# Loading the output projection in runs of 4 KiB, with the attention output laid out to match

## The chip, the cores and the metric

The kernel runs on one core of one Trainium2 chip. The metric is the device time of one execution in microseconds (us); medians of several runs are given. In the lines of the profile, PE is TensorE's matmul unit, DVE is VectorE, ACT is ScalarE, and SPq is the queue of SyncE, which issues the loads. The loads are carried by 16 DMA engines.

## The reference, cut to what matters

```python
xn  = layernorm(x)                               # x: 4 x 1 x 512
q   = (xn @ wq) as (4, 32 heads, 1, 128)
p   = softmax(q . k_cache * 128**-0.5)           # k_cache: 4 x 32 x 8192 x 128, bf16
o   = p . v_cache                                # v_cache: the same size
out = x + o.reshape(4, 1, 4096) @ wo + ffn(xn)   # wo: 4096 x 512
```

One decode step for a batch of 4: K and V together are 537 MB, wo is 4.19 MB, and all of it is read once.

## The kernel before: the parts that the argument touches

K and V come in tiles of 2 MiB through a pool of nine slots, all issued from one queue, one K and one V tile for each of the 128 (head, batch) pairs. After the four batches of a head, its output stands in PSUM with one row per batch and group; it is copied to SBUF, *turned* so that the 128 values of the head lie on the partitions, divided by the row sums, and later multiplied with the 128 rows of wo that belong to the head.

```python
def load_wo(half):                       # two tiles of 16 heads; runs of 512 elements = 1 KiB
    n = H // 2
    t_ = slot()
    nc.sync.dma_start(out=t_[:].rearrange("p (h e) -> p h e", h=n),
                      in_=A_wo[half * n * P:(half + 1) * n * P, :].rearrange("(h p) e -> p h e", p=P))
    wo_t.append(t_)
...
def fin_2(h):                            # the turn: 4 fp32 matmuls with 128 stationary columns
    o_sb = osb.pop(h)
    xps = psX.tile([P, B], dt.float32, name="xps")
    for u in range(NV):
        mm(xps[:], o_sb[:, u * Dh:(u + 1) * Dh], ident_f[:, u:P:QB], start=(u == 0))
    nc.vector.tensor_tensor(out=otn[:, h, :], in0=xps[:], in1=rcp.pop(h)[:], op=ALU.mult)

def wo_mm(h):                            # one product per head, added up in PSUM
    w = wo_t[h // (H // 2)][:].rearrange("p (h e) -> p h e", e=D)
    mm(yo_ps[0:B, :], otn[:, h, :], w[:, h % (H // 2), :], start=False)
...
        if 0 <= mf < M and mf % B == B - 1:
            fin_2(mf // B)
            wo_ready = mf // B + 1       # products of wo that may be issued
```

## Time and profile before

| what | before |
|---|---|
| time, median of 6 runs | 1297.78 us (1297.59 to 1297.96) |
| share of the span in which PE was busy | 85% |
| read from HBM | 550.77 MB |
| rate in most slices | 429 to 434 GB/s |
| rate in slices 36 and 37 (the wo loads) | 403 and 419 GB/s |
| PE passes in the turn of all heads | 256, 253 ns each |

So there are two numbers to read from any run of it: **when the last K tile lands**, and **how long the chain behind it is**. The lines of the profile itself stand in the prediction.

### The profile page before, as it was taken

What the parts mean: (1) busy time and instruction counts of PE and PEld (TensorE: products, weight loads), DVE (VectorE), ACT (ScalarE), POOL (GpSimd) and SP (SyncE); (2) the same over time, 40 slices, a digit from 0 to 9 for tenths busy, and PEclk for the clock granted to TensorE, in tenths of its full rate; (3) what the DMA queues carried; (4) which work ended last, traced back from release to release, by engine and by line L of the source; (5) the groups of instructions that cost most, each with busy time, mean ns of one, the idle gap of its engine ahead of it and who ended that gap; (6) DMA issues with size and microseconds to landing.
All of it is one profiled execution on the core that took longest, in us unless ns stands there. A gap on an engine that the chain in (4) does not pass through costs nothing.

```text
span 1295.9 us, 11245 instructions
## 1 busy us (share of the span) xinstructions
PE 1095.1 (85%) x4676; PEld 423.2 (33%) x4676; DVE 693.3 (54%) x887; ACT 48.5 (4%) x102; POOL 5.6 (0%) x11
## 2 busy tenths in 40 slices
PE   5889888888888888888888888888888888886987
PEld 2343333333333333333333333333333333332333
DVE  7635554554554565555565455555555555544542
ACT  1000000000000000000000000000000000000000
POOL 1000000000000000000000000000000000000000
PEclk8989999999999999999999999999989989998999
DMA  9999999999999999999999999999999999999997
GB/s 396 429 430 432 431 429 431 431 431 430 430 432 430 430 430 431 431 429 432 432 428 429 434 430 429 431 431 431 431 431 431 430 430 431 430 403 419 432 429 305
DMA packets 42210, 551.49 MB, mean 426 GB/s; under 512 B 4264, under 2 KB 8368, under 8 KB 8880
## 3 DMA queue, kind: packets, MB, share of 16 engines
q1 hardware_dynamic: 42160, 550.79, 99.6%
q8 instruction: 36, 0.59, 0.2%
q14 instruction: 14, 0.11, 0.0%
HBM read 550.77 MB, written 0.00 MB: 425 GB/s over the span
## 4 chain that ended last, share of the span: by engine, by line
DMA 91%; PE 5%; DVE 3%; issue 0%; SPq 0%; ACT 0%; DVEq 0%; ACTq 0%
DMA slot<-in_A_k_cache_dram 86%; DMA slot<-in_B_w_up_dram 3%; DVE kt L256 3%; DMA slot<-in_A_v_cache_dram 3%; PE oacc L74 2%; PE sps L74 2%; PE mps L74 1%; PE xps L74 0%; SPq L97 0%; PE mps L278 0%; SPq L89 0%; DVE mx L272 0%; DVE res L388 0%; DVE yfx L227 0%; ACT o_sb L313 0%
## 5 line engine op out<-in xcount | busy, mean ns | idle before, releaser
L256 DVE STREAM_TRANSPOSE kt<-slot 128x1024 uint32<-128x1024 uint32 x512 | 593.5, 1212 | 284.8 <-DMA slot<-in_A_k_cache_dram 284.8
L74 PE MATMUL sps<-kt,zq 128*128 128x512 bf16 x2048 | 572.1, 416 | 179.0 <-DVE kt L256 165.6
L74 PEld LDWEIGHTS <-zq 128*128 128x128 bf16 x2048 | 208.8, 103 | 532.0 <-issue 361.4
L302 DVE RECIPROCAL rcp<-mps 128x4 f32<-128x4 f32 x32 | 5.8, 183 | 160.9 <-PE mps L74 160.9
L272 DVE TENSOR_REDUCE mx<-sps 128x1 f32<-128x512 f32 x32 | 22.1, 692 | 45.1 <-PE sps L74 45.1
L281 DVE TENSOR_REDUCE nm<-mps 128x4 f32<-128x64 f32 x32 | 7.2, 225 | 50.0 <-PE mps L278 50.0
L74 PE MATMUL xps<-ident_f,o_sb 128*128 128x4 f32 x256 | 33.1, 253 | 0.7 <-ACT o_sb L313 0.7
L74 PEld LDWEIGHTS xps<-ident_f,o_sb 128*128 128x128 f32 x256 | 31.1, 192 | 1.2 <-ACT o_sb L313 1.2
L247 DVE COPY zq<-qt 32x16 bf16<-32x16 bf16 x128 | 23.5, 183 | 1.3
L322 DVE TENSOR_TENSOR otn<-xps,rcp 128x4 bf16<-128x4 f32 x32 | 5.2, 162 | 34.1 <-PE xps L74 34.1
L313 ACT COPY o_sb<-oacc 128x512 f32<-128x512 f32 x32 | 18.7, 585 | 20.6 <-PE oacc L74 20.5
L74 PE MATMUL oacc<-slot,pt__1952 128*4 128x512 bf16 x64 | 14.6, 379 | 0.0
L74 PE MATMUL oacc<-slot,pt__3394 128*4 128x512 bf16 x64 | 14.6, 379 | 0.0
L74 PE MATMUL oacc<-slot,pt__6498 128*4 128x512 bf16 x64 | 14.6, 379 | 0.0
L74 PE MATMUL oacc<-slot,pt__922 128*4 128x512 bf16 x64 | 14.6, 379 | 0.0
L74 PE MATMUL oacc<-slot,pt__2158 128*4 128x512 bf16 x64 | 14.6, 379 | 0.0
L74 PE MATMUL oacc<-slot,pt__3188 128*4 128x512 bf16 x64 | 14.6, 379 | 0.0
L74 PE MATMUL oacc<-slot,pt__4424 128*4 128x512 bf16 x64 | 14.6, 379 | 0.0
L74 PE MATMUL oacc<-slot,pt__5248 128*4 128x512 bf16 x64 | 14.6, 379 | 0.0
L74 PE MATMUL oacc<-slot,pt__6282 128*4 128x512 bf16 x64 | 14.6, 379 | 0.0
L74 PE MATMUL oacc<-slot,pt__371 128*4 128x512 bf16 x64 | 14.6, 379 | 0.0
L74 PE MATMUL oacc<-slot,pt__1128 128*4 128x512 bf16 x64 | 14.6, 379 | 0.0
(204 smaller groups left out, 636.8 us busy)
## 6 DMA issues: line engine op xcount, KB each, us to landing
slot<-in_A_k_cache_dram SPq DMA_DIRECT2D x128, 2048.0 KB, 38.4
slot<-in_A_v_cache_dram SPq DMA_DIRECT2D x127, 2048.0 KB, 38.8
slot<-in_A_wq_dram SPq DMA_DIRECT2D x2, 2048.0 KB, 9.4
slot<-in_A_wo_dram SPq DMA_DIRECT2D x2, 2048.0 KB, 28.8
slot<-in_A_v_cache_dram SPq DMA_DIRECT2D x4, 512.0 KB, 28.0
slot<-in_B_w_gate_dram SPq DMA_DIRECT2D x1, 1792.0 KB, 38.2
slot<-in_B_w_up_dram SPq DMA_DIRECT2D x1, 1792.0 KB
slot<-in_B_w_down_dram SPq DMA_DIRECT2D x1, 1792.0 KB, 34.0
```

Source lines behind the costliest of these rows:

```text
L74: nc.tensor.matmul(out_ap, lhsT=lhsT, rhs=rhs, start=start, stop=True, skip_group_check=True, **kw)
L247: nc.vector.tensor_copy(out=zq[h % 2][a * QB:(a + 1) * QB, :, :, XO + a * QB].rearrange("p b (j r) -> p r j b", r=2), in_=qt[a * QB:(a + 1 ...
L256: nc.vector.transpose(out=kt[:].bitcast(dt.uint32).rearrange("p (j t r) -> p t j r", j=2, r=QB), in_=src.rearrange("p (t j r) -> p t j r", ...
L272: nc.vector.reduce_max(out=mx[:], in_=s_ps[h][:], axis=AX.X)
L281: nc.vector.tensor_reduce(out=nm[:], in_=mps[:, 0:P].rearrange("p (a x g r) -> p x a g r", a=NQ, x=B, r=2)[:, :, :, :, 0], axis=AX.XY, op= ...
L302: nc.vector.reciprocal(out=r_[:], in_=mps[:, P:P + B])
L313: nc.scalar.copy(out=o_sb[:], in_=o_acc[h % 2][:])
L322: nc.vector.tensor_tensor(out=otn[:, h, :], in0=xps[:], in1=rcp.pop(h)[:], op=ALU.mult)
```

## The change

The intent is larger runs for wo: a partition gets four neighbouring rows of wo, 4 KiB, instead of one of 1 KiB. Partition p then holds the rows 4p to 4p+3 of a block of 512 rows, which belong to head p // 32 of the block and to its elements 4(p mod 32) to +3. The attention output has to lie the same way: 32 partitions for each of four heads, every fourth element per product. So the turn makes 16 narrow matmuls in place of 4 wide ones, and the products of four heads can start only when all four are there.

```diff
-        nc.sync.dma_start(out=t_[:].rearrange("p (h e) -> p h e", h=n),
-                          in_=A_wo[...].rearrange("(h p) e -> p h e", p=P))
+        nc.sync.dma_start(out=t_[:].rearrange("p (k c e) -> p k (c e)", c=4, e=D),
+                          in_=A_wo[...].rearrange("(k p c) e -> p k (c e)", p=P, c=4))
 ...
-        xps = psX.tile([P, B], dt.float32, name="xps")
-        for u in range(NV):
-            mm(xps[:], o_sb[:, u * Dh:(u + 1) * Dh], ident_f[:, u:P:QB], start=(u == 0))
-        nc.vector.tensor_tensor(out=otn[:, h, :], in0=xps[:], in1=rcp.pop(h)[:], op=ALU.mult)
+        xps = psX.tile([P, 4, B], dt.float32, name="xps")
+        k, hh = divmod(h, 4)
+        q0, q1 = hh * QB, (hh + 1) * QB
+        for c in range(4):
+            for u in range(NV):
+                mm(xps[q0:q1, c, :], o_sb[:, u * Dh + c:(u + 1) * Dh:4], ident_f[:, u:P:QB], start=(c == 0 and u == 0))
+        nc.vector.tensor_tensor(out=otn[q0:q1, k * 4:k * 4 + 4, :], in0=xps[q0:q1],
+                                in1=rcp.pop(h)[q0:q1, :].unsqueeze(1).to_broadcast([QB, 4, B]), op=ALU.mult)
 ...
-            wo_ready = mf // B + 1
+            wo_ready = mf // B // 4 * 4 + (4 if mf // B % 4 == 3 else 0)
```

## The prediction

> **What bounds the kernel now.** I read the page first: the slices, the chain that ended last, and the DMA issues.
>
> ```profile
> span 1295.9 us, 11245 instructions
> ...
> DMA  9999999999999999999999999999999999999997
> GB/s 396 429 430 432 431 429 431 431 431 430 430 432 430 430 430 431 431 429 432 432 428 429 434 430 429 431 431 431 431 431 431 430 430 431 430 403 419 432 429 305
> DMA packets 42210, 551.49 MB, mean 426 GB/s; under 512 B 4264, under 2 KB 8368, under 8 KB 8880
> ...
> DMA 91%; PE 5%; DVE 3%; issue 0%; SPq 0%; ACT 0%; DVEq 0%; ACTq 0%
> ...
> slot<-in_A_wo_dram SPq DMA_DIRECT2D x2, 2048.0 KB, 28.8
> ```
>
> The reader is to see that the 16 DMA engines are busy in every slice and that the chain is 91% DMA: 550 MB have to come in, nearly all of it K and V, and they do so at 431 GB/s. PE is 85% busy, but its idle time is spent waiting for transposed K, which waits for the loads. Two dips stand out in the rate: the first slice (start-up) and slices 36 and 37 (403 and 419), where the two wo tiles of 2 MiB are loaded. The change cannot touch the first. So I looked at the second with a table of busy time in stretches of 4 us around the wo loads (its last two columns are the DMA engines' busy share and GB/s), and at what the issuing queue did then.
>
> ```profile
> 1130.00:1150.00 20.00, 16.21 (x69) 5.93 (x67) 11.76 (x18) 1.36 (x3) 0.00 (x0) 1.00 1.01 431
> ...
> 1154.00:1158.00 4.00, 3.15 (x19) 1.82 (x18) 1.00 (x3) 0.00 (x0) 0.00 (x0) 1.00 1.03 404
> 1158.00:1162.00 4.00, 3.45 (x9) 1.23 (x9) 3.88 (x4) 0.00 (x0) 0.00 (x0) 0.58 0.84 290
> 1162.00:1166.00 4.00, 4.00 (x19) 1.47 (x18) 0.00 (x0) 0.00 (x0) 0.00 (x0) 0.99 0.99 381
> ...
> 1174.00:1178.00 4.00, 4.00 (x15) 1.40 (x14) 2.67 (x6) 0.00 (x0) 0.00 (x0) 0.79 1.11 379
> ```
>
> ```profile
> 1128.83 0.39 SPq L236 DMA_DIRECT2D slot<-in_A_wo_dram  x1
> 1131.53 29.54 SPq L97 DMA_DIRECT2D slot<-in_A_k_cache_dram  x1
> 1161.16 0.38 SPq L106 DMA_DIRECT2D slot<-in_A_v_cache_dram  x1
> 1161.64 0.39 SPq L236 DMA_DIRECT2D slot<-in_A_wo_dram  x1
> 1162.12 14.25 SPq L97 DMA_DIRECT2D slot<-in_A_k_cache_dram  x1
> ```
>
> The lasting rate is 431 GB/s. The eight stretches from 1150 to 1182 us moved 424, 404, 290, 381, 430, 420, 379 and 397: together 323 GB/s short, times 4 us, over 431, is **3.0 us lost** around wo. That is the ceiling of the gain. 0.16 x 4 = 0.64 us of it, in 1158 to 1162, is engines with nothing to do (share 0.84): the K load issued behind the first wo load took 29.54 us to issue against the usual 0.33, so the queue behind wo ran nearly dry. The other 2.36 us are engines that were busy and moved less.
>
> The end matters as much, because a single core's time ends with it. The timeline of the last 16 us:
>
> ```profile
> 1278.99 1.03 PE L74 MATMUL xps<-ident_f,o_sb 128*128 128x4 f32 x8
> ...
> 1280.28 0.38 PE L74 MATMUL yo_ps<-slot,otn 128*4 128x512 bf16 x1 [0.25 <-DVE otn L322]
> ...
> 1284.21 6.21 PE L74 MATMUL oacc<-slot,pt__6913 128*4 128x512 bf16 x32 [0.32 <-DMA slot<-in_A_v_cache_dram]
> ...
> 1291.16 1.05 PE L74 MATMUL xps<-ident_f,o_sb 128*128 128x4 f32 x8 [0.73 <-ACT o_sb L313]
> ```
>
> From 1284.21 on PE never waits for data again: 32 matmuls with V, a copy by ACT, the 8 passes that turn the last head, one DVE multiply, one product with wo, the cast and the store. Every nanosecond added to the last head's turn or to the wo products behind it is on the path. What is added for head 30 (at 1278.99) has 0.32 us to spare.
>
> **What the Trainium skill says.** "DMA: Bandwidth & Descriptors", section "Why small descriptors are slow (HBM only)", gives a fixed overhead of about 3 cycles per packet beside 32 bytes per cycle. An estimate from it: 1 KiB takes 35 cycles instead of 32, 9% more; 4 KiB 131 instead of 128, 2% more. On 9.73 us of wo (4.19 MB at 431 GB/s) that is 0.9 and 0.2 us. The trace agrees in kind, but its loss of 2.36 us is larger, so I use the trace. "TensorE: Matmul & The Clock Gate", section "LDWEIGHTS (loading the stationary operand)", has the load as columns / 1.2 ns, whatever the rows: 107 ns for 128 columns, 27 for 32. The trace agrees for 128: eight passes in 1.03 us, the last lasting 0.25, leave 0.78 / 7 = 111 ns per pass. No row of this trace has 32 fp32 columns. The same page, "Weight-path perf modes", says that the fast weight load needs 128 weights that are not fp32; these are fp32, so going to 32 columns should lose no fast load. "TensorEngine Tiling (Array Packing)", section "Key Properties", says that a change of tiling mode drains TensorE; the kernel already goes between 128-column and 4-column matmuls without a wait beyond some tenths of a us, so I charge nothing for it.
>
> **The change part by part.** Load: each wo tile goes from 2048 runs of 1 KiB to 512 of 4 KiB. Per engine, both tiles are 4096 / 16 = 256 packets; 2.36 us / 256 = 9.2 ns extra per packet. With 64 packets that leaves 0.6 us, so 1.77 us come back. The dry queue should go too, as K's issue has a quarter of wo's packets ahead of it: 0.64 us. **Gain 2.4 us**, and it reaches the end, since the transposes after wo still wait for K (4.40 us before the one at 1225.94, 5.15 us before the one at 1264.84).
>
> The turn of a head: 4 fp32 matmuls (8 passes) with 128 stationary columns become 16 (32 passes) with 32 columns at a stride of 4 elements. The build confirms 16 where there were 4, with the other engines' sequences unchanged. At 111 ns the old passes take 0.89 us. For the new ones the shortest spacing in the trace is about 27 ns (24 matmuls with 16 columns moving, 0.76 us less the last one's time), and the strided bf16 weights of the FFN take 3.52 / 56 = 63 ns. I choose the middle, 45 ns: 32 x 45 = 1.44 us, so **+0.55 us per head** (0 to +1.1). For 32 heads that is 18 us of PE, but all save the last two lie where PE idles for K: its matmuls for the scores have 179 us of idle time ahead of them. DVE's multiply writes 32 x 16 instead of 128 x 4; it lasts 162 ns now, and 12 more elements per partition are an estimated 0.01 to 0.02 us.
>
> The wo products: four heads now have to be there before any of the four is used, so those of heads 28, 29 and 30 move behind head 31. One costs (1.24 - 0.38) / 4 = 0.215 us from the run of five at 1207.80. **At the end +0.65 us.** In return head 30's product and PE's wait of 0.25 us for it leave 1280.28, 0.47 us in all, about what that head's longer turn adds; the 0.32 us of slack takes the rest.
>
> Sum: -2.4 + 0.0 (head 30) + 0.55 (head 31) + 0.65 = **-1.2 us**, so 1297.76 - 1.2 = 1296.6 us.
>
> **The rivals.** First, the turn becomes slow: if narrow strided loads do not overlap with matmuls, a pass takes its whole 250 ns, 32 of them 8 us. That would be +7 us per head, +14 at the end, 1310 us. Against it: the 4-column loads of the V products already run ahead of matmuls, 3.11 us for 16. In the middle it would still be mostly hidden, since PE has some 2.5 us to spare in each 9.7 us that a K and a V load need, and a head is turned once in four of those. Second, the loads gain nothing: 4 KiB runs may be as slow as 1 KiB ones, or the loss may be of two large tiles ahead of K in the queue, not of the run length. Then only the end's cost is left: 1299. For it: nothing in the middle of the trace has 4 KiB runs. Against it: the last V is loaded in four parts of 4 KiB runs and its slice still moved 429 GB/s before the ramp down. Third, the whole 3.0 us come back and the turn costs nothing: 1295.4.
>
> **Range and chances.** The best case is -3.0 + 0.65 = -2.35 us; a poor one is -1.0 + 0.65 + 1.1 + 0.3 (head 30 beyond its slack) = +1.05. So 1295.2 to 1298.8 holds it 8 times in 10. 2% are 26 us, nine times the ceiling of the gain, so faster is all but excluded; slower would need something worse than the first rival. I give 0.005, 0.985 and 0.01.
>
> **What would show it.** In the profile after: packets under 2 KB down by 4096 and those under 8 KB by 3072; slices 36 and 37 near 430 GB/s; no issue of K lasting tens of us behind wo; the group of the turn with 1024 passes at a spacing near 45 ns; at the end four wo products in a row, and from the last V matmul to the end about 1.2 us more than the 5.5 before (1290.4 to 1295.9). It is wrong if the rate around wo stays low, or if the turn's passes are spaced 100 ns or more.

## More of the kernel before

The program has one core, so there is no second die to compare with.

The kernel is as fast as its loads until the last K tile has landed; from there a chain of about 31 us (transpose, scores, softmax, products with V, turn, wo, store) leads to the end.

## The result, and the profile after

The changed kernel takes **1300.03 us** (median of 6 runs, 1299.62 to 1300.59) against 1297.78 before: 2.25 us longer, where 1.2 us less had been forecast. The ratio is 1.0018 (1.0005 to 1.0031). Ratios here are the mean time of one kernel's fast runs over that of the other's of the same rounds, so not quite the ratio of the medians.

The page of the changed kernel:

```profile
span 1298.8 us, 12782 instructions
...
GB/s 394 430 430 431 431 429 431 430 431 430 430 431 430 431 430 431 431 429 432 428 431 432 429 431 430 432 430 430 429 431 430 430 430 431 431 427 430 431 430 238
DMA packets 39144, 551.59 MB, mean 425 GB/s; under 512 B 4264, under 2 KB 4272, under 8 KB 5808
...
q8 instruction: 42, 0.69, 0.2%
...
L74 PE MATMUL xps<-ident_f,o_sb 128*32 128x4 f32 x1024 | 66.7, 202 | 0.7 <-ACT o_sb L314 0.7
```

Everything asked of the load came true: 4096 short packets are gone, and the dip in slices 36 and 37 has vanished (427 and 430). Yet the last slice moved 238 GB/s instead of 305, in a longer span. The instruction count rose by 1,537, of which 1,536 are on PE, and with it the packets on the queue marked "instruction": 42 instead of 36. This line became the key. (Of the two such queues, q8 fetches for PE and q14 for GpSimd: section 4 adds instructions to one engine at a time, and the packets rise on that queue alone.)

The issuing queue behind wo, in the changed kernel:

```profile
1130.52 0.39 SPq L237 DMA_DIRECT2D slot<-in_A_wo_dram  x1
1132.29 6.07 SPq L97 DMA_DIRECT2D slot<-in_A_k_cache_dram  x1
...
1149.33 11.81 SPq L97 DMA_DIRECT2D slot<-in_A_k_cache_dram  x1
```

K's issue behind wo is still slow, but 6.07 and 11.81 us rather than 29.54 and 14.25.

Now the two numbers. In the timeline of the kernel before, the DVE line marks the landing of the last K (its transposes start when it lands), the ACT line the copy after the last product with V, and the PE line the last product with wo:

```profile
1264.84 4.62 DVE L256 STREAM_TRANSPOSE kt<-slot 128x1024 uint32<-128x1024 uint32 x4 [5.15 <-DMA slot<-in_A_k_cache_dram]
...
1290.52 0.58 ACT L313 COPY o_sb<-oacc 128x512 f32<-128x512 f32 x1 [15.36 <-PE oacc L74]
...
1292.47 0.38 PE L74 MATMUL yo_ps<-slot,otn 128*4 128x512 bf16 x1 [0.26 <-DVE otn L322]
```

The same timeline of the changed kernel:

```profile
1265.23 4.62 DVE L257 STREAM_TRANSPOSE kt<-slot 128x1024 uint32<-128x1024 uint32 x4 [5.09 <-DMA slot<-in_A_k_cache_dram]
...
1290.88 0.58 ACT L314 COPY o_sb<-oacc 128x512 f32<-128x512 f32 x1 [15.33 <-PE oacc L74]
...
1291.51 2.08 PE L74 MATMUL xps<-ident_f,o_sb 128*32 128x4 f32 x32 [0.73 <-ACT o_sb L314]
...
1293.87 1.87 PE L74 MATMUL yo_ps<-slot,otn 128*4 128x512 bf16 x4 [0.27 <-DVE otn L327]
...
1295.77 0.68 DVE L395 CAST res<-yo_ps 4x512 bf16<-4x512 f32 x1 [1.96 <-PE yo_ps L74]
```

The last K lands 0.39 us *later* (1265.23 to 1264.84), though the dip is gone. From there to the ACT copy both take the same (25.65 and 25.68 us). From the ACT copy to the end of the span it is 7.9 us instead of 5.4. So this profiled run, the slowest of its six, lost 0.4 us in the loads and 2.5 us in the chain. Two questions follow: what became of the gain in the loads, and why does the chain cost more than the 1.2 us that were forecast for it?

### The profile page after: what moved, and what is told of

Same layout as the page of the kernel before. It is cut to its first block, busy times and chain, and to the rows that moved or that the text cites. A ratio compares the mean times of both kernels' runs of the same rounds, so it can differ in the third digit from the quotient of the medians.

```text
span 1298.8 us, 12782 instructions
## 1 busy us (share of the span) xinstructions
PE 1143.9 (88%) x5444; PEld 465.9 (36%) x5444; DVE 695.8 (54%) x887; ACT 48.5 (4%) x102; POOL 5.6 (0%) x11
## 4 chain that ended last, share of the span: by engine, by line
DMA 67%; PE 24%; DVE 8%; issue 1%; SPq 0%; ACT 0%; DVEq 0%; ACTq 0%
DMA slot<-in_A_k_cache_dram 64%; PE oacc L74 11%; PE sps L74 10%; DVE kt L257 7%; DMA slot<-in_B_w_up_dram 3%; PE xps L74 2%; PE mps L74 1%; PE mps L279 0%; PE yo_ps L74 0%; DVE otn L327 0%; SPq L97 0%; ACT p__7257 L289 0%; SPq L89 0%; DVE pt__7271 L296 0%; DVE nm L282 0%
## 5 line engine op out<-in xcount | busy, mean ns | idle before, releaser
L74 PE MATMUL sps<-kt,zq 128*128 128x512 bf16 x2048 | 585.6, 432 | 133.8 <-DVE kt L257 125.9
L74 PEld LDWEIGHTS <-zq 128*128 128x128 bf16 x2048 | 211.6, 105 | 491.5 <-issue 327.1
L74 PE MATMUL xps<-ident_f,o_sb 128*32 128x4 f32 x1024 | 66.7, 202 | 0.7 <-ACT o_sb L314 0.7
L74 PEld LDWEIGHTS xps<-ident_f,o_sb 128*32 128x32 f32 x1024 | 63.9, 156 | 1.8 <-ACT o_sb L314 1.2
L327 DVE TENSOR_TENSOR otn<-xps,rcp 32x16 bf16<-32x16 f32 x32 | 5.5, 170 | 68.6 <-PE xps L74 68.6
```

The source lines that it names most:

```text
L74: nc.tensor.matmul(out_ap, lhsT=lhsT, rhs=rhs, start=start, stop=True, skip_group_check=True, **kw)
L327: nc.vector.tensor_tensor(out=otn[q0:q1, k * 4:k * 4 + 4, :], in0=xps[q0:q1], in1=rcp.pop(h)[q0:q1, :].unsqueeze(1).to_broadcast([QB, 4, B ...
```

## The experiments

Eleven kernels were run, in three groups, each with 4 or 5 timed runs, beside the kernel before on the same chip (its median was 1297.69 us in the first two groups and 1297.71 in the third; 9 or 10 runs). The intervals of the ratios here are wide, some 0.13% or 1.7 us to each side, so an argument from a smaller difference rests on this: on one chip no run of the one kernel overlaps with a run of the other. A warning first: three of them use a load and a layout that do not belong together, and the comparison with the reference passed them as correct all the same. The attention term is small beside x in these inputs, so a pass there does not vouch for the layout of wo; that of the changed kernel I checked by its indices only.

### 1. The load alone

```diff
 # the kernel before, with only this (wrong on purpose: the turn stays as it was)
-  ... "p (h e) -> p h e" ... "(h p) e -> p h e"
+  ... "p (k c e) -> p k (c e)" ... "(k p c) e -> p k (c e)"
```

> Only the wo load has 4 KiB runs; the turn and the wo products are as before, so the result is wrong on purpose. Theory A (a load counts as landed when the slowest of its 16 engines is done; in the kernel before, much of the dip around wo was fast engines waiting for slow ones, which costs the end nothing): the K landing near 1215 us comes 1.0 to 1.8 us earlier than before, the time falls by 1.0 to 1.8 us, and the rate falls to half some 8 us before the last load ends. Rival B (all of the lost rate counts): the time falls by 2.4 to 3.0 us. Rival C (run length does nothing for the end): 0.

Measured: 1296.92 us (1296.79 to 1296.97), 0.77 less than before. The last K lands 0.86 us earlier than before:

```profile
1263.98 4.62 DVE L257 STREAM_TRANSPOSE kt<-slot 128x1024 uint32<-128x1024 uint32 x4 [5.15 <-DMA slot<-in_A_k_cache_dram]
```

So most of the 3.0 us of lost rate was not on the path. To see why, read the rate at the end, in 40 slices of 0.8 us from 1264 to 1296 us (shares in tenths, then GB/s). The kernel before:

```profile
DMA  9998998998999999999899899996531000000000
GB/s 389 471 451 348 430 512 369 430 512 369 389 492 410 410 471 410 410 451 451 369 425 471 333 389 425 415 410 251 205 128 51 0 0 0 0 0 0 3 3 0
```

With the load alone changed:

```profile
DMA  9999999999999989999975655564300000000000
GB/s 492 389 410 492 389 410 492 410 410 430 451 389 430 471 353 405 492 384 389 497 312 225 261 220 241 230 246 189 128 36 0 0 0 0 0 0 5 0 0 0
```

Before, all engines work until about 1285.6 and then finish within some 3 us of each other. With 4 KiB runs about half of them are done by 1280.8, and the others go on alone, for 4.8 us at about 237 GB/s and then slower to the end. The engines are not level. The trace records when each of the 16 engines of a load has reported. For the load that landed near 1112 us, ahead of wo, the first report came 6.9 us ahead of the last in the kernel before and 6.8 us in this one. For the last K it was 3.4 us in the kernel before, and 7.7 us in this one: **the dip around wo had levelled the engines**. A tile counts as landed with its slowest engine, so fast engines that run dry in the dip cost nothing. Counted over all 16 engines, the mean lead over the slowest fell from 3.3 us (landing at 1150.9) to 1.8 us (1191.3) in the kernel before. By that estimate about half of the dip, 1.5 of 3.0 us, was fast engines waiting. Theory A's mechanism holds; its range of 1.0 to 1.8 us was still a little high. Whether the 0.77 us come from the longer runs themselves or from a queue that no longer runs dry was not tested apart.

### 2. The turn and the products alone

```diff
 # the changed kernel, with the load of the kernel before (wrong on purpose)
```

> Only the turn of the heads and the grouping of the wo products are changed, wo is loaded in 1 KiB runs as before; wrong on purpose. Tail as in the changed kernel: about 1.0 us for the last turn, 1.5 us for four products at half clock, 0.3 for head 30, so +2.5 to +2.9. Theory A adds that the 1,536 more PE instructions cost DMA time to be fetched (6 fetches of 16 KiB of about 0.95 us each, on engines that carry K and V): K landings near 1147 us 0.5 to 0.9 us later than before, so +3.0 to +3.8 in all. Rival D (instruction fetches are hidden): landings unchanged, +2.5 to +2.9.

Measured: 1300.95 us (1300.51 to 1301.69), +3.26. The last K lands 1.10 us later than before, and the four products take:

```profile
1265.94 4.62 DVE L256 STREAM_TRANSPOSE kt<-slot 128x1024 uint32<-128x1024 uint32 x4 [5.09 <-DMA slot<-in_A_k_cache_dram]
...
1294.62 1.02 PE L74 MATMUL yo_ps<-slot,otn 128*4 128x512 bf16 x4 [0.27 <-DVE otn L326]
```

1.02 us here, 1.87 us in the changed kernel, for the same four products. The table of busy time in stretches tells why; its third column from the right is the granted clock. The changed kernel from 1293 to 1295 us:

```profile
1293.00:1295.00 2.00, 1.73 (x13) 0.85 (x13) 0.18 (x1) 0.00 (x0) 0.00 (x0) 0.50 0.00 0
```

The same stretch with the turn and the products alone:

```profile
1293.00:1295.00 2.00, 1.73 (x25) 1.44 (x25) 0.18 (x1) 0.00 (x0) 0.00 (x0) 1.00 0.00 0
```

At the half clock a product of 512 columns takes 0.43 us instead of 0.22 (the distance of the weight loads for the last products in the two timelines). "TensorE: Matmul & The Clock Gate", section "Part 1: The HAM clock gate", says that the clock falls to half after an idle window of some 3.4 us which runs freely, so that the same kernel meets it at different places. The trace agrees on the length and the place: its spells at half clock last 3.4 us or a multiple, and it was full in one profiled execution and half in the other. It does not show an idle window: in the 3.4 us before the clock fell, at 1292.88 us in the changed kernel, PE waited for 0.73 us only.

The time lies within Theory A's range of +3.0 to +3.8 us, but in part by luck: the range had counted on the half clock and on 0.3 us for head 30. The profiled run had the full clock, and its parts add up: 1.10 us in the landing, 1.03 in the last turn and 0.66 in the products are 2.79 us, and its span is 2.8 us longer (1298.7 to 1295.9).

### 3. The end alone

```diff
 # the kernel before; heads 28 to 31 only: the narrow turn, products after head 31
+        if h < H - 4:
+            return fin_2_old(h)
```

> As the kernel before, but the last four heads have the narrow turn and their four wo products come together at the end; 1 KiB load, so wrong for those heads. Both theories: +2.2 to +2.9 us from the end alone, and K landings as before within 0.3 us. The difference to the run with the narrow turn for all heads is the cost of the other 28 heads: 0.5 to 0.9 by theory A, 0 by rival D.

Measured: 1299.45 us (1299.29 to 1300.32), +1.76: below the range of 2.2 to 2.9, which had counted on the half clock. Its profiled run is the slow one of 1300.32, with four products in 1.83 us. The last K lands as before (0.13 us later):

```profile
1264.97 4.62 DVE L256 STREAM_TRANSPOSE kt<-slot 128x1024 uint32<-128x1024 uint32 x4 [5.15 <-DMA slot<-in_A_k_cache_dram]
```

By the medians the other 28 heads therefore cost 1300.95 - 1299.45 = 1.50 us, of which 0.97 (1265.94 - 1264.97) are in the landing of the last K. Their longer turns lie where PE idles, so by rival D they should have cost nothing.

### 4. Instructions without the change

These four kernels leave wo, the turn and the end alone and add work that nobody reads ahead of the turns of heads 0 to 27. `xps5` is the turn's PSUM tile made 512 columns wide, and `qt_as_128x512` stands for a view of a tile at hand.

```diff
 # more_24, more_96: n = 24 or 96
+            for _ in range(n):
+                mm(xps5[0:4, 8:12], ident[:, 0:4], ident[:, 0:4], start=True)
 # long_20
+            for _ in range(20):
+                mm(xps5[0:4, :], ident[:, 0:4], qt_as_128x512, start=True)
 # pool_192
+            for _ in range(192):
+                nc.gpsimd.memset(pad_t[0:1, 0:1], 0.0)
```

> The kernel before, with 24 tiny matmuls (4 columns in, 4 out, a result nobody reads) ahead of the turn of each of the heads 0 to 27: 1,344 more PE instructions, some 1 to 1.5 us of PE per head, nothing added at the end. Theory A (their fetching costs the DMA engines time): about 5 more fetches of 16 KiB, the last K lands 0.7 to 1.2 us later, the time rises by as much. Rival D (fetching is hidden): 0, within 0.2.

> The same with 96 tiny matmuls per head: 5,376 more PE instructions, some 3 to 6 us of PE per head. Theory A: 21 more fetches, the last K 3.5 to 4.8 us later, and the landing times of the 16 engines spread wider before wo. Rival D: 0. Rival E (PE's longer work frees the buffers later, and so delays the loads): 0 to several us, and the same with few long matmuls.

> 20 matmuls with 512 columns (0.216 us each, 4.3 us of PE per head) instead of the 96 tiny ones: as much PE time as the run with 96, but only 1,120 more instructions, as few as the run with 24. Theory A: +0.6 to +1.1 us, as the run with 24. Rival E: as the run with 96.

> 5,376 one-element memsets on GpSimd, which is otherwise idle, in place of the tiny matmuls: as many instructions as the run with 96, no PE time at all. Theory A: their fetches ride on the DMA engines too, +1 to +5 us, depending on which engines carry them. Rivals D and E: 0.

| kernel | added instructions | more fetch packets | time | against before |
|---|---|---|---|---|
| 24 tiny matmuls per head | 1,344 on PE | 6 | 1298.79 us | +1.10 |
| 20 long matmuls per head | 1,120 on PE | 5 | 1298.71 us | +1.02 |
| 96 tiny matmuls per head | 5,376 on PE | 21 | 1301.60 us | +3.91 |
| 192 memsets per head | 5,376 on GpSimd | 42 | 1315.04 us | +17.35 |

The kernel before has these instruction packets (count, MB, share of the engines' time):

```profile
q8 instruction: 36, 0.59, 0.2%
q14 instruction: 14, 0.11, 0.0%
```

With 96 tiny matmuls per head:

```profile
GB/s 395 429 432 429 431 430 430 430 431 427 434 427 432 430 429 432 428 432 430 430 430 430 430 431 429 432 429 431 430 430 432 429 431 428 431 388 417 431 430 297
...
q8 instruction: 57, 0.93, 0.3%
```

With the memsets:

```profile
GB/s 395 430 429 430 431 429 430 430 430 430 430 431 431 430 431 429 430 430 430 429 430 431 431 430 431 431 430 430 430 431 431 431 430 431 430 211 418 430 431 294
...
q14 instruction: 56, 0.46, 0.1%
```

**The fetches cost the end time.** As an average, 1.10 / 6, 1.02 / 5 and 3.91 / 21 are 0.18, 0.20 and 0.19 us per fetch of 16 KiB for PE, and 17.35 / 42 is 0.41 us per fetch of 8 KiB for GpSimd. The two runs with few fetches took the times that Theory A expected. The other two missed it in part: with 96 tiny matmuls the last K lands 2.54 us later where 3.5 to 4.8 had been expected, and the memsets cost 17.35 us where 1 to 5 had been expected.

**For PE the cost comes in steps, one for every eighth fetch.** In the steady part a load lands every 4.85 us. With 96 tiny matmuls the fetches number 1, 9, 17, 25, 33, 41, 49 and 57 are each followed by a landing that is 1.28 to 1.40 us late; away from the loads of wo and the FFN no other is followed by more than 0.41 us. The kernel before has 36 fetches. The run with 24 tiny matmuls has 42, and number 41 comes at 1261.7 us: the K before the last lands 0.10 us later than in the kernel before, the last one 1.24 us later.

```profile
1255.17 4.62 DVE L256 STREAM_TRANSPOSE kt<-slot 128x1024 uint32<-128x1024 uint32 x4 [3.70 <-DMA slot<-in_A_k_cache_dram]
1266.08 4.62 DVE L256 STREAM_TRANSPOSE kt<-slot 128x1024 uint32<-128x1024 uint32 x4 [6.29 <-DMA slot<-in_A_k_cache_dram]
```

With the 20 long ones number 41 comes at 1287.8 us, too late for the last K (0.08 us later than before). It delays the last V, by 0.97 us, and PE waits for it:

```profile
1264.92 4.62 DVE L256 STREAM_TRANSPOSE kt<-slot 128x1024 uint32<-128x1024 uint32 x4 [5.15 <-DMA slot<-in_A_k_cache_dram]
...
1290.13 1.02 PE L74 MATMUL oacc<-slot,pt__7473 128*4 128x512 bf16 x4 [0.48 <-DMA slot<-in_A_v_cache_dram]
```

I read this as the fetches going round eight engines: a fetch delays a tile only where it falls on the engine that is already last. So 36 to 40 fetches should cost the same. The end alone has 37 and lands 0.13 us later; 38 to 40 were not run. 41 and 42 fetches are one step more than 36, and 57 are three: 1.02, 1.10 and 3.91 / 3 = 1.30 us a step.

PE's own time is not the reason. The groups of added matmuls, for the run with 20 long ones and for the run with 96 tiny ones:

```profile
L74 PE MATMUL xps<-qt,ident 128*4 128x512 bf16 x560 | 125.4, 379 | 0.0
```

```profile
L74 PE MATMUL xps<-ident 128*4 128x4 bf16 x2688 | 71.1, 164 | 0.0
```

The long ones keep PE busy for 125 us more and cost as little as the 24 tiny ones; this rules out rival E for this size. The memsets use no PE time and cost most. The times when the engines reported tell why. With the memsets, for the load that landed at 1129.8 us, 15 engines had reported at least 17.9 us before it and one came alone at the end; GpSimd's fetches evidently all ride on one engine, which then holds up every tile. Of the other 15, seven are furthest ahead (20.4 to 24.6 us before the last) and eight trail them (17.9 to 18.9), which fits eight engines for PE's fetches. The records name no engine, so that the lag of a fetch falls on the very engine that carried it is argued, not shown.

The last thing to read in the two rate lines is the dip at wo. Wo is loaded in the same 1 KiB runs in both, but slices 36 and 37 fell to 388 and 417 with 57 fetches and to 211 and 418 with the memsets. Over slices of 32.8 us the latter is (220 + 13) x 32.8 / 431 = 17.7 us of lost rate, the whole delay that one engine had gathered. In the same way the dip is 3.0 us in the kernel before and 4.3 us with 57 fetches. Over it the mean lead of the engines over the slowest fell by 1.5, 3.3 and 16.3 us. **What differs between these dips is the lag between the engines, not the price of short runs**; the other 1.0 to 1.5 us are in all three. With 4 KiB runs and a lag of 7 us there is no dip at all, so, as I read it, the lag shows as a dip only where the queue runs dry.

### 5. The changed kernel again, and an attempt at the clock

```diff
 # warm_end: the changed kernel, last head only
+            for _ in range(3):
+                mm(xps5[0:4, :], ident[:, 0:4], qt_as_128x512, start=True)
```

> The changed kernel once more, on this chip beside the others: +2.0 to +2.9 us against before. The four wo products at the end take about 1.0 us where the granted clock is full and 1.9 us where it has fallen to half; single runs therefore lie up to 0.9 us apart.

> The changed kernel with three long matmuls that nobody reads in PE's wait of 0.73 us for the last copy by ACT, so that PE is kept busier ahead of the last turn. If the half clock at the end comes from PE doing too little in the stretch before, the clock stays full more often: 0.3 to 0.8 us less than the changed kernel on the same chip, with the four products in about 1.0 us. If the turn's own passes are what counts as idle, no gain: 0 to 0.2 us more, for the tail of the long matmuls.

Measured: 1299.68 us for the changed kernel again (1299.51 to 1300.21, +1.97), and 1300.08 us (1299.77 to 1300.20) with the three long matmuls. The first is just under the 2.0 to 2.9 us expected, and the second is no gain. The test was a miss: the added matmuls ran interleaved with the last products of V, so PE waited 0.73 us for ACT as before. Its profiled run, its fastest at 1299.77 us, did have the full clock, with the four products in 1.02 us; one run does not tell whether that was more than chance. Whether filling that wait would hold the clock stays open.

### 6. A version that keeps the gain

For heads 0 to 27 ACT copies each head into its place among four, so that one stationary block of 128 columns holds 32 columns of each; 16 matmuls then turn four heads, as many as before the change. Heads 28 to 31 and their rows of wo stay in the old form, so that the end is as short as before. The second version also keeps the copy in bf16, which halves the passes. In words, against the changed kernel:

```diff
-  for each head:           16 matmuls with 32 fp32 columns
+  for each four heads:     16 matmuls with 128 columns, otn = xps * rcp for all four at once
+  wo of heads 0 to 27 in 4 KiB runs, of heads 28 to 31 in 1 KiB runs; last four heads turned as before
+  grouped_bf16: the copy and the identity in bf16
```

> A correct kernel that should beat both: wo in 4 KiB runs for heads 0 to 27, whose outputs are turned four heads at once with 128 columns (16 matmuls for four heads, as many as before), and the last four heads and their wo rows as before. Theory A: no added instructions, the end as before, so the gain of the load alone remains: -1.0 to -1.8 us against before. Rival B: -2.0 to -2.7.

> The grouped kernel with the turn in bf16 instead of fp32: half the passes, each shorter. The last head's turn falls from 1.05 us to some 0.3 to 0.5, and some 350 fewer PE instructions save one fetch (0.2 us): 0.6 to 1.0 us less than the grouped kernel, so 1295.8 to 1296.3 us. If the end were set by the loads alone it would stay at 1296.8.

Measured: 1296.82 us (1296.69 to 1296.96, -0.87) and 1296.03 us (1295.96 to 1296.18, -1.68). The first keeps the gain of the load alone (-0.77) and nothing else, as the explanation asks; the -1.0 to -1.8 expected was too much in the same way as in section 1. The second, as expected within 1295.8 to 1296.3 us, also shortens the last turn from 1.05 us to 0.26, which is the whole difference between the two:

```profile
1290.50 0.26 PE L74 MATMUL xps<-ident,o_sb 128*128 128x4 bf16 x4 [0.68 <-ACT o_sb L327]
```

The fetch that it saves (35 instead of 36) brought nothing: its last K lands at 1264.25 us, that of the first at 1264.09. Both beat the two kernels; the intervals of their ratios (0.9993, 0.9981 to 1.0006, and 0.9987, 0.9975 to 1.0000) are wide, but no single run of either was slower than 1296.96 and none of the kernel before faster than 1297.57.

## Why the prediction was wrong

The time stayed within 2%, as forecast, and the place where the change would be felt was right. What the prediction had named as signs of its being right came true, save the spacing of the passes and the time behind the last V, and neither of its signs of being wrong appeared. The sum had the wrong sign. Its terms:

- **"Gain 2.4 us, and it reaches the end": this is the step that failed.** It took the lost rate for lost time. The rate did come back, to 427 and 430, but the load alone was worth 0.77 us. By the estimate above about half of the dip was fast engines waiting for slow ones, and the landing of K goes by the slowest. The split into 0.64 us idle and 2.36 us "busy and moved less" fell with it: with the same 1 KiB runs the dip was 17.7 us deep once one engine lagged.
- **A term was missing: the fetching of the instructions.** The prediction charged the earlier turns nothing, since PE has idle time. PE has; the DMA engines that fetch 1,536 more instructions have not. This cost 0.97 us in the landing of the last K and 1.50 us in the median, between the run with the end alone (37 fetches) and that with the turn of all heads (42). In the traces it is one step. In the changed kernel the loads land 0.86 us earlier than before up to 1244 us, as with the load alone. Fetch number 41 comes at 1248.7 us, and the next load lands 1.48 us late, which ends in the 0.39 us of loss at the last K. With the turn and the products alone, number 41 comes at 1250.0 us, and the next load is 1.19 us late. Five fetches at the average price, 0.95 us, come near the 0.97 by chance, since the other four cost nothing there. The remaining 0.5 us is not explained. More frequent half clock at the end would do it, but was not shown: the profiled run of the turn alone, at the full clock, took 1300.51 us, about 1.1 us more than the four faster runs of the end alone (1299.29 to 1299.47), whose clock at the end is not on record.
- **The turn of the last head, +0.55 us: measured +1.03** (from its first pass to DVE's multiply 2.12 us instead of 1.09). The passes are about 61 ns apart (2.08 us less the last one's 0.20, over 31), at the upper end of the 27 to 63 ns that I had between; the middle was the wrong choice where a strided example stood at 63.
- **The wo products, +0.65 us: right at full clock** (1.07 us from the first product to the cast with the turn and the products alone, against 0.41 before), but +1.49 in the profiled run of the changed kernel, where the clock had fallen to half. The prediction did not think of the clock, although the narrow turn leaves PE little to do just before the products.
- **Head 30, 0.0: right.** From the last K's landing to the last ACT copy it is 25.65 us against 25.68.

Together the medians give -0.77 (load) + 1.76 (end) + 1.50 (the other heads) = +2.49 us; measured were +2.25 and, on the chip of the third group, +1.97. The parts were run alone, so they need not add up to the tenth. The rivals fared no better: the second, "4 KiB runs gain nothing", came nearest in its number (1299), but for another reason than its own, as the load alone did gain.

## What to carry to other kernels

In a kernel bound by its loads, measure a gain by when the last tile *lands*, not by the rate: a tile waits for the slowest of its 16 engines, and a dip in the rate may only be the fast ones waiting. Instructions are loads too: PE instructions that hide behind idle time still have to be fetched by engines that carry the data. Here the few fetches more that PE needed cost nothing but for one, which cost over 1 us at once. The same number of instructions was more than four times as dear on GpSimd as on PE (17.35 to 3.91 us). A change that makes the middle cheaper must leave the chain behind the last load alone; splitting off the last four heads did that here.

## What the Trainium skill lacked or had wrong

- "Runtime: NRT & Kernel Launch", section "Instruction fetch mechanics", has the fetch in 16 KiB blocks and its cost "mostly hidden". The first half agrees for PE (36 packets, 0.59 MB); the packets on the other instruction queue are 8 KiB (56 in 0.46 MB). The cost is not hidden where the DMA engines are the bound: 0.18 to 0.20 us of the kernel's time for each of PE's on average, in steps of 1.28 to 1.40 us for every eighth with 96 tiny matmuls per head, and 0.41 us for each of GpSimd's.
- "DMA: Bandwidth & Descriptors" says that a bulk load runs at the pace of its slowest engine, which agrees, and names two engines that are usually slower. It does not say that engines which also fetch instructions fall ever further behind the others in a steady stream; here the first reported 1.6 us before the last near 68 us and 6.9 us before it near 1112 us, and with the memsets one engine was at least 17.9 us behind all others.
- The same page's section "Why small descriptors are slow (HBM only)" led to an estimate of 0.9 us minus 0.2 us for going from 1 KiB to 4 KiB runs; the load alone was worth 0.77 us. The page was nearer than my reading of the dip, but no run here shows that its cause, a fixed cost per packet, is the one at work.
- "TensorE: Matmul & The Clock Gate", section "LDWEIGHTS (loading the stationary operand)", leads to an estimate of 27 ns for 32 columns. For 32 fp32 columns at a stride of four elements the passes were 61 ns apart; that section has no figure for strided or fp32 columns. It is no floor for every small matmul here: with 96 tiny ones per head, 4 bf16 columns each, they ran 25 ns apart. Which of stride and fp32 it was, no run separates.
